# Four single-bank PSUM tiles, another walk over layer 2's odd rows, a pad and another warm-up in an attention and feed-forward kernel

## The chip, the core and the metric

The kernel runs on one core of one Trainium2 chip. The metric is the device time of one execution in microseconds (us), the median of several runs. TensorE (PE) multiplies matrices and writes its results to PSUM, which here has eight banks of 512 fp32 words per partition; VectorE (DVE), ScalarE (ACT) and GpSimd (POOL) do elementwise work, and DVE and ACT empty PSUM; the queue of SyncE (SP) issues the transfers.

## What is computed

```
attention: 4 batches x 8 heads, 576 tokens, head width 64
  scores = q k^T / 8;  keep those >= row max - tau;  softmax over what is kept;  times v
x = the heads side by side                       # 2304 tokens x 512
layer 1: h = x w_in (512 -> 2048); g = h if h >= 1, 0 if h <= -1, else (h + 1)^2 / 4; y = g w_out
layer 2: h = y w_in2 (512 -> 2048); g = s * max(h, 0)^2 + b; out = g w_out2
```

## The kernel before

Every operand of the large matrix products is split into a high and a low part, and each product is done as three matmuls (high by high, high by low, low by high).

A list scheduler that runs on the host writes out the order of all instructions of all engines: each task has engines that may do it, a cost on each, a priority, the tasks that it reads from, and, where it uses PSUM, a group. A group gets a bank when its first product is put in the order and gives it back when its last eviction is. The products of the feed-forward part are also chained in one fixed order on PE ("pe order").

The program has three parts. Attention (to about 500 us) works on half heads: PE makes scores (L576) into double PSUM tiles, DVE takes row maxima (L631), ACT, DVE and POOL do the threshold and the softmax, PE transposes and multiplies by v. Beside and after it the first hidden units of layer 1 are done directly ("plain slices", up to L1018, whose last joins read PSUM). Then come nine steps of three passes over three blocks of 768 tokens: one pass for the second half of layer 1 and two for layer 2.

A step has two halves. gemm1 (L1223) makes eight slices of hidden units for its block from seven products in the order 1, 5, 6, 3, 2, 7, 4 (a scheme of Strassen's type), each 384 columns wide and six matmuls long for each of four pairs of slices. Products are evicted by `copied` (ACT L1127 or DVE L1128) or `joined` (DVE L1131) and shaped by the activation into the slices G, a high and a low part each, in the array pr. gemm2 sums the eight slices into the output: in layer 1 by L1263 (eight groups of 384 columns), in layer 2 by L1299 (six tiles of 128 tokens, 512 columns wide, 6 x 8 x 3 = 144 matmuls for a block, 864 in all). Its rows are the eight slices, first the even ones 0, 2, 4, 6, then the odd ones 1, 3, 5, 7, since gemm1 finishes them in that order; for each row all the tiles are served. In L1299 the stationary operand is G from pr, and the moving one a unit of weights of 2048 bytes in lr, lh or pr; the odd rows read units in lh and pr.

PSUM has two double tiles ps2_0 and ps2_1 (banks 0 to 3), two single tiles ps1_0 and ps1_1 (4 and 5) and a third double tile ps3 (6 and 7), which late in attention is replaced by two single ones. Semaphores guard a whole tile: a write to one half of a double tile waits for reads of the other half, and a read of one half for writes of the other.

At the start nothing can be multiplied until the first inputs land, and PE does matmuls on an identity meanwhile: "fills" (L1397), which the scheduler puts wherever PE would stand idle, and a warm-up of 27 transposes (L781) into ps3 from a copy of the identity that POOL makes.

Of the kernel before, what the change touches and what calls it, by code (L numbers as in the profile page):

```python
# [34 lines left out]
AHEAD = 1  # L35
WARM = 9

# [26 lines left out]
NJ = 4  # L64
BLOCKS = ((0, 768), (768, 768), (1536, 768))
BT = 768
# [18 lines left out]
PR_BYTES = O_EXTRA + UNIT * (NPLACE - NLEFT - NTAIL - NFREE)  # L85
PF_BYTES = 8 * BT


# [263 lines left out]
def mm_ns(n):  # L352
    return 0.443 * n + 5
# [12 lines left out]
def attention_then_ffn(tc, qk, v, tau, w1, w2, s2, b2, out):  # L366
# [53 lines left out]
    ap_ = at_cm.__enter__()  # L420
    ident_r = ap_.tile([128, 128], F32R, name="identr")
    hs_b = [Buf("LF", 1280 * i, TM) for i in range(NH)]
# [9 lines left out]

    ps2 = [pp.tile([128, 2, 512], F32, name=f"ps2_{i}") for i in range(2)]
    ps1 = [pp.tile([128, 512], F32, name=f"ps1_{i}") for i in range(2)]
# [7 lines left out]
    def two_banks():  # L442
        pb["cm"].__exit__(None, None, None)
        pb["cm"] = tc.tile_pool(name="psb", bufs=1, space=bass.MemoryType.PSUM)
        q = pb["cm"].__enter__()
        bank[6:8] = [q.tile([128, 512], F32, name=f"ps4_{i}")[:, :] for i in range(2)]

    E = [ap_.tile([128, S], F32, name=f"e{i}") for i in range(NE)]
# [16 lines left out]
    def consts():  # L465
        make_identity(nc, ident)
        nc.gpsimd.tensor_copy(out=ident_r, in_=ident)
        for c, x in ((half, 0.5), (part_c, 1.0 / S), (tiny_c, 1e-9)):
            nc.vector.memset(c, x)
# [305 lines left out]
    def warm_up():  # L775

        g = Group([(7,)])

        def mm():
            for _ in range(3 * WARM):  # L780
                nc.tensor.transpose(bank[7][:, 0:128].bitcast(F32R), ident_r, ident_r)  # L781

        add([("pool", 1260.0, consts)], (0, 0), w=["ident"])
        add([("pe", WARM * 213.0, mm)], (0, 0), r=["ident"], w=[("bank", g)], group=g)

# [23 lines left out]
    def final():  # L809
        late["md"].__exit__(None, None, None)  # L810
        xg.__exit__(None, None, None)
        late["cm"] = tc.tile_pool(name="final", bufs=1, side="right")
        q = late["cm"].__enter__()
        arena["PR"] = q.tile([128, PR_BYTES // 4], F32R, name="pr")
        arena["PF"] = q.tile([128, PF_BYTES // 4], F32, name="pf")

# [236 lines left out]
    class Pass:  # L1053
# [6 lines left out]
        def product(self, p, j):  # L1060
            return ORDER.index(p) * self.nj + j
# [121 lines left out]
    def gemm1(P, T, first):  # L1183
# [17 lines left out]
        for p in ORDER:  # L1201
# [6 lines left out]
            for j in range(nj):  # L1208
                if p == 1:
                    A[j] = Group(ANY8)  # L1210
                elif p == 5:
                    Bk[j] = Group(ANY8)
# [12 lines left out]

                product(pe, 6 * mm_ns(n), mm, u.keys() + r.keys(), g)
                even, odd = even_b[j], odd_b[j]
# [52 lines left out]
    def gemm2(P, t0, T):  # L1280
# [26 lines left out]
        for i in range(ny):  # L1307
            sums(i)
        for f in rows:
            for i in range(m):  # L1310
                ku = P.unit[P.out(f, 0)].keys() + P.unit[P.out(f, 1)].keys()
                kg = G_b[f].keys(128 * i, 128) + G_b[f].keys(BT + 128 * i, 128)
                product(prs[i][0], 3 * mm_ns(n), lambda f=f, i=i: mm(f, i, gy[i][0]), ku + kg, gy[i][0])
        for i in range(m):
# [50 lines left out]
    layer1 = [t for t in sch.tasks[first:] if t.alts[0][0] != "sp"]  # L1365
    after([t for t in layer1 if t.alts[0][0] == "pe"][:-8], lambda: None, "pe order")
    passes = [Pass(n, layer, f0, nj, 11 * sum(p[2] for p in PASSES[:n])) for n, (layer, f0, nj) in enumerate(PASSES)]
    work = [P.jobs() for P in passes]
# [32 lines left out]
    with tc.manual_schedule():  # L1401
        for t in order:
            t.fn[2]()
    late["cm"].__exit__(None, None, None)
# [66 lines left out]
```

## Time and profile before

| | |
|---|---|
| device time, median of 3 runs | 1081.29 us (1079.51 to 1081.51) |
| device time of the profiled execution | 1079.24 us |
| its span | 1077.4 us |
| PE busy over the span | 1052.1 us (98%), 6491 matmuls |
| DVE busy | 802.2 us (74%) |
| ACT busy | 704.6 us (65%) |
| POOL busy | 428.3 us (40%) |
| DMA, mean over the span | 186 GB/s |

The span is what the hardware profiler saw from the first instruction to the last; the execution's own time is 1.84 us longer. Busy times are those of one execution and overlap between engines.

### The profile page before, as it was taken

The numbers are of one execution on the slowest core, as the hardware profiler recorded it, in microseconds if no ns is written. First come the engines' busy times: TensorE is split into PE (matmuls) and PEld (weight loads), VectorE is DVE, ScalarE is ACT, GpSimd is POOL, SyncE is SP. The second block draws the span as 40 slices with busy tenths as digits, with TensorE's granted clock in tenths as the row PEclk, the third lists the DMA queues.
The fourth block names the chain that finished last, engine by engine and source line by source line (L and its number), as shares of the span: only waits on it lengthen the run. The fifth ranks groups of instructions, "written<-read, shape, count | busy, mean of one in ns | idle before, by whom it ended". The sixth has DMA issues, their size and how long they took to land.

```text
span 1077.4 us, 19033 instructions
## 1 busy us (share of the span) xinstructions
PE 1052.1 (98%) x6491; PEld 925.3 (86%) x6491; DVE 802.2 (74%) x1596; ACT 704.6 (65%) x1322; POOL 428.3 (40%) x653
## 2 busy tenths in 40 slices
PE   9989999999999999999999999999999999999998
PEld 6556877788888898899999999998989889898996
DVE  7988998797887899757888979786796726356372
ACT  7998888898998988734535446265684626346260
POOL 5766767889898978332302111120100101000000
PEclk9999999999999999999999999999999999999999
DMA  5654455565647665599856499843638951140112
GB/s 169 201 156 148 137 184 193 187 199 174 184 137 217 182 198 169 188 355 365 297 173 224 129 307 348 309 168 131 230 128 279 343 174 63 40 137 20 60 30 87
DMA packets 105120, 199.95 MB, mean 186 GB/s; under 512 B 11328, under 2 KB 33344, under 8 KB 105024
## 3 DMA queue, kind: packets, MB, share of 16 engines
q1 hardware_dynamic: 105024, 198.75, 55.9%
q8 instruction: 51, 0.84, 0.3%
q14 instruction: 45, 0.37, 0.1%
HBM read 134.61 MB, written 64.09 MB: 184 GB/s over the span
## 4 chain that ended last, share of the span: by engine, by line
PE 71%; ACT 8%; DVE 6%; issue 2%; POOL 2%; DMA 1%; DVEq 0%; ACTq 0%; POOLq 0%
PE ps L1223 23%; PE ps L1299 18%; PE ps L1263 9%; PE ps L928 5%; PE ps L961 4%; PE ps L695 2%; PE ps L733 2%; PE ps L1009 2%; PE ps L585 2%; ACT p L674 2%; DVE p L639 1%; ACT e L634 1%; ACT pt L687 1%; PE ps L576 1%; PE ps L734 1%
## 5 line engine op out<-in xcount | busy, mean ns | idle before, releaser
L1223 PE MATMUL ps<-pr,lr 128*128 128x384 f32 x816 | 144.7, 336 | 0.0
L1223 PEld LDWEIGHTS ps<-pr,lr 128*128 128x128 f32 x816 | 141.7, 188 | 0.4 <-DVE lg L1131 0.2
L639 DVE SCALAR_TENSOR_TENSOR p<-ps,stt,e 128x576 f32<-128x576 f32 x144 | 116.3, 812 | 21.7 <-ACT e L634 16.8
L1223 PE MATMUL ps<-lr 128*128 128x384 f32 x672 | 122.2, 336 | 0.6 <-DVE lg L1131 0.3
L1223 PEld LDWEIGHTS ps<-lr 128*128 128x128 f32 x672 | 116.7, 188 | 3.1 <-issue 1.4
L631 DVE TENSOR_REDUCE stt<-ps 128x1 f32<-128x576 f32 x144 | 105.8, 749 | 18.2 <-PE ps L585 9.3
L928 PE MATMUL ps<-xh,lr 128*128 128x320 f32 (+1 forms) x512 | 112.6, 299 | 0.2 <-DVE lf L938 0.2
L634 ACT ACTIVATE e<-ps,stt 128x576 f32<-128x576 f32 x144 | 105.9, 751 | 10.4 <-DVE stt L631 9.9
L1299 PE MATMUL ps<-lr,pr 128*128 128x512 f32 x432 | 102.6, 397 | 0.2
L674 ACT ACTIVATE p<-p,stt 128x576 f32<-128x576 f32 (+3 forms) x112 | 93.3, 838 | 12.8 <-DVE stt L658 11.7
L555 DVE TENSOR_TENSOR pr<-lg,pr 128x768 fp32r<-128x768 f32 x71 | 69.2, 978 | 41.6 <-POOL pr L838 26.5
L1299 PEld LDWEIGHTS ps<-lr,pr 128*128 128x128 f32 x432 | 80.5, 188 | 21.0 <-DVE pf L1128 1.4
L1131 DVE TENSOR_TENSOR lg<-lg,ps 128x384 f32<-128x384 f32 (+1 forms) x104 | 56.3, 560 | 47.7 <-PE ps L1299 31.3
L695 PE MATMUL ps<-ident,p 128*128 128x128 f32 x576 | 82.7, 275 | 7.3 <-ACT pt L687 5.2
L928 PEld LDWEIGHTS ps<-xh,lr 128*128 128x128 f32 x512 | 85.1, 188 | 2.9 <-DVE lk L880 0.8
L961 PE MATMUL ps<-g,lr 128*128 128x256 f32 (+1 forms) x600 | 87.1, 297 | 0.0
L687 ACT COPY pt<-ps 128x512 f32<-128x512 f32 x143 | 79.9, 591 | 5.4 <-PE ps L695 5.1
L695 PEld LDWEIGHTS ps<-ident,p 128*128 128x128 f32 x576 | 66.0, 140 | 19.6 <-ACT pt L687 5.5
L1127 ACT COPY lg<-ps 128x384 f32<-128x384 f32 (+1 forms) x107 | 49.3, 494 | 50.8 <-PE ps L1223 44.2
L961 PEld LDWEIGHTS ps<-g,lr 128*128 128x128 f32 x600 | 80.7, 189 | 0.0
L928 PE MATMUL ps<-xl,lr 128*128 128x256 f32 (+1 forms) x256 | 75.3, 294 | 0.0
L733 PE MATMUL ps<-pt,vr 128*64 128x256 f32 (+1 forms) x512 | 69.1, 412 | 0.7 <-ACT pt L687 0.6
(128 smaller groups left out, 2268.1 us busy)
## 6 DMA issues: line engine op xcount, KB each, us to landing
wd<-lh SPq DMA_DIRECT2D x118, 256.0 KB, 4.0
lr<-wd SPq DMA_DIRECT2D x108, 256.0 KB, 5.5
lk<-in_w_dram SPq DMA_DIRECT2D x48, 512.0 KB, 4.5
vr<-in_v_dram SPq DMA_DIRECT2D x32, 320.0 KB, 3.4
r<-in_qk_dram SPq DMA_DIRECT2D x32, 288.0 KB, 3.1
lg<-y1T SPq DMA_DIRECT2D x6, 1536.0 KB, 7.4
lk<-in_w_dram SPq DMA_DIRECT2D x32, 256.0 KB, 3.8
r<-in_qk_dram SPq DMA_DIRECT2D x16, 304.0 KB, 4.2
```

What stands on the lines that cost most here:

```text
L631: add([("dve", 665, lambda: nc.vector.tensor_reduce(out=nm[:, x:x + 1], in_=Sv(), axis=AX.XY, op=ALU.min))], at(pr, "min"), r=[kg], w=[ks[ ...
L634: add([("act", 624, lambda: nc.scalar.activation(out=ev, in_=Sv(), func=AF.Exp, bias=nm[:, x:x + 1], scale=-1.0))], at(pr, "exp"), r=[kg, ...
L639: nc.vector.scalar_tensor_tensor(out=p[:, x * S:x * S + S].rearrange("p (a c) -> p a c", a=2), in0=Sv(), scalar=nthr[:, x:x + 1], in1=ev, ...
L674: nc.scalar.activation(out=p[i:j, o:o + w], in_=p[i:j, a:a + w], func=AF.Identity, scale=rc[i:j, x:x + 1], bias=un[i:j, x:x + 1])
L687: add([("act", actp_ns(n), lambda: [nc.scalar.copy(out=a, in_=b) for a, b in zip(dst, src())]), ("dve", dve_ns(n), lambda: [nc.vector.tens ...
L695: nc.tensor.transpose(bank[g.banks[0]][:, j * 128:(j + 1) * 128], p[:, c0 + j * 128:c0 + (j + 1) * 128], ident)
L733: nc.tensor.matmul(o[64 * x:64 * x + 64, 0:n], vr[:, c:c + D], PT[:, x, k, c0:c0 + n], start=(k == 0), stop=False)
L928: nc.tensor.matmul(o, a, x, start=(n == 0), stop=(n == 11))
L961: nc.tensor.matmul(o, a[:, c], x, start=(f == 0 and n == 0), stop=(f == nf - 1 and n == 2))
L1223: nc.tensor.matmul(o, a, y, start=(i == 0 and p in (1, 5, 2)), stop=(i == 5), skip_group_check=p not in (1, 5, 2))
L1263: nc.tensor.matmul(o, w, x, start=(f == rows[0] and s == 0), stop=(f == rows[-1] and s == 2))
L1299: nc.tensor.matmul(o, a, y, start=(f == rows[0] and s == 0), stop=(f == rows[-1] and s == 2))
```

## The change

It has four parts.

1. The double tiles ps2_0 and ps2_1 get a pool of their own. When the order has come past every task whose group may use a bank below 4 as part of the earlier program (scores, plain slices), `four_banks` closes that pool and opens four single tiles ps5_0 to ps5_3 in the same banks. In the first block, product 1 may only use banks 4 to 7, and product 5 waits for the switch (key "four").
2. In layer 2's gemm2 the even rows are walked as before. The odd rows are walked tile by tile: for each tile of 128 tokens its four odd rows one after the other, twelve matmuls.
3. The array pf is 288 bytes longer. In the built program this moves pr from byte 163808 of each partition to 163520.
4. The warm-up is five fp32 matmuls on the identity itself; its cost in the scheduler's plan stays (1917 ns). The copy of the identity, and its cast on POOL, are gone. Fills that the plan starts before 4500 ns are not written out.

```diff
--- before.py
+++ after.py
@@ -33,7 +33,7 @@
 NSX, NV = 4, 2
 
 AHEAD = 1
-WARM = 9
+WARM, WARM_NS, FILL_FROM = 5, 1917.0, 4500.0
 
 FILL = 200000.0
 NE, NP, NST, NH, LEAD = 2, 3, 4, 3, 3
@@ -84,6 +84,7 @@
 O_EXTRA = 8 * BT * 2 * NJ
 PR_BYTES = O_EXTRA + UNIT * (NPLACE - NLEFT - NTAIL - NFREE)
 PF_BYTES = 8 * BT
+PAD = 288
 
 
 
@@ -418,7 +419,6 @@
     garr = [xp_.tile([128, 2 * TM], F32R, name=f"g{i}") for i in range(NGL)]
     at_cm = tc.tile_pool(name="attn", bufs=1, side="right")
     ap_ = at_cm.__enter__()
-    ident_r = ap_.tile([128, 128], F32R, name="identr")
     hs_b = [Buf("LF", 1280 * i, TM) for i in range(NH)]
     c_b = [Buf("LF", 3840 + 1280 * i, TM) for i in range(NH)]
     ye_b = [Buf("LF", 7680 + 1280 * i, TM) for i in range(2)]
@@ -430,7 +430,9 @@
     yD = dp.tile([NT, DM], F32, name="yd")
     wD = dp.tile([11 * sum(nj for _, _, nj in PASSES), 128, 512], F32, name="wd")
 
-    ps2 = [pp.tile([128, 2, 512], F32, name=f"ps2_{i}") for i in range(2)]
+    pair_cm = tc.tile_pool(name="pairs", bufs=1, space=bass.MemoryType.PSUM, side="right")
+    pairs = pair_cm.__enter__()
+    ps2 = [pairs.tile([128, 2, 512], F32, name=f"ps2_{i}") for i in range(2)]
     ps1 = [pp.tile([128, 512], F32, name=f"ps1_{i}") for i in range(2)]
 
     pb = {"cm": tc.tile_pool(name="psa", bufs=1, space=bass.MemoryType.PSUM)}
@@ -445,6 +447,12 @@
         q = pb["cm"].__enter__()
         bank[6:8] = [q.tile([128, 512], F32, name=f"ps4_{i}")[:, :] for i in range(2)]
 
+    def four_banks():
+        pair_cm.__exit__(None, None, None)
+        late["singles"] = tc.tile_pool(name="singles", bufs=1, space=bass.MemoryType.PSUM, side="right")
+        q = late["singles"].__enter__()
+        bank[0:4] = [q.tile([128, 512], F32, name=f"ps5_{i}")[:, :] for i in range(4)]
+
     E = [ap_.tile([128, S], F32, name=f"e{i}") for i in range(NE)]
     P = [ap_.tile([128, 2 * S], F32, name=f"p{i}") for i in range(NP)]
 
@@ -464,7 +472,6 @@
 
     def consts():
         make_identity(nc, ident)
-        nc.gpsimd.tensor_copy(out=ident_r, in_=ident)
         for c, x in ((half, 0.5), (part_c, 1.0 / S), (tiny_c, 1e-9)):
             nc.vector.memset(c, x)
 
@@ -777,11 +784,11 @@
         g = Group([(7,)])
 
         def mm():
-            for _ in range(3 * WARM):
-                nc.tensor.transpose(bank[7][:, 0:128].bitcast(F32R), ident_r, ident_r)
+            for _ in range(WARM):
+                nc.tensor.matmul(bank[7][:, 0:128], ident, ident, start=True, stop=True)
 
         add([("pool", 1260.0, consts)], (0, 0), w=["ident"])
-        add([("pe", WARM * 213.0, mm)], (0, 0), r=["ident"], w=[("bank", g)], group=g)
+        add([("pe", WARM_NS, mm)], (0, 0), r=["ident"], w=[("bank", g)], group=g)
 
     def attention():
         next_of(prep)
@@ -812,7 +819,7 @@
         late["cm"] = tc.tile_pool(name="final", bufs=1, side="right")
         q = late["cm"].__enter__()
         arena["PR"] = q.tile([128, PR_BYTES // 4], F32R, name="pr")
-        arena["PF"] = q.tile([128, PF_BYTES // 4], F32, name="pf")
+        arena["PF"] = q.tile([128, (PF_BYTES + PAD) // 4], F32, name="pf")
 
     def after(tasks, fn, key, r=()):
         sw = add([("host", 1, fn)], (0, aidx[0] + 1), r=r, w=[key])
@@ -1207,7 +1214,7 @@
             split(T, lambda r=r: r(0, T), lambda r=r: r(BT, T), val[p][0], val[p][1], r.keys(0, T), r.keys(BT, T), sp, pairs_of)
             for j in range(nj):
                 if p == 1:
-                    A[j] = Group(ANY8)
+                    A[j] = Group(ANY if first else ANY8)
                 elif p == 5:
                     Bk[j] = Group(ANY8)
                 g = A[j] if p in (1, 6, 7, 4) else Bk[j] if p in (5, 3) else Group(ANY8)
@@ -1223,7 +1230,7 @@
                             nc.tensor.matmul(o, a, y, start=(i == 0 and p in (1, 5, 2)), stop=(i == 5), skip_group_check=p not in (1, 5, 2))
                             i += 1
 
-                product(pe, 6 * mm_ns(n), mm, u.keys() + r.keys(), g)
+                product(pe, 6 * mm_ns(n), mm, u.keys() + r.keys() + ["four"] * (first and p == ORDER[1]), g)
                 even, odd = even_b[j], odd_b[j]
                 row, at_, n_ = {1: (even, 0, 0), 5: (odd, n, 0), 6: (even, n, 0), 3: (even, n, 1), 7: (odd, n, 1), 2: (even, 0, 1), 4: (odd, 0, 0)}[p]
                 (joined if n_ else copied)(g, n, lambda row=row, at_=at_: row(at_, n), row.keys(at_, n), po)
@@ -1306,11 +1313,12 @@
 
         for i in range(ny):
             sums(i)
-        for f in rows:
-            for i in range(m):
-                ku = P.unit[P.out(f, 0)].keys() + P.unit[P.out(f, 1)].keys()
-                kg = G_b[f].keys(128 * i, 128) + G_b[f].keys(BT + 128 * i, 128)
-                product(prs[i][0], 3 * mm_ns(n), lambda f=f, i=i: mm(f, i, gy[i][0]), ku + kg, gy[i][0])
+        walk = [(f, i) for f in rows[:NJ] for i in range(m)]
+        walk += [(f, i) for i in range(m) for f in rows[NJ:]]
+        for f, i in walk:
+            ku = P.unit[P.out(f, 0)].keys() + P.unit[P.out(f, 1)].keys()
+            kg = G_b[f].keys(128 * i, 128) + G_b[f].keys(BT + 128 * i, 128)
+            product(prs[i][0], 3 * mm_ns(n), lambda f=f, i=i: mm(f, i, gy[i][0]), ku + kg, gy[i][0])
         for i in range(m):
             g, y = gy[i]
             po = prs[i][2]
@@ -1364,6 +1372,7 @@
         l1_out(q, f, f0, f1, gs[n])
     layer1 = [t for t in sch.tasks[first:] if t.alts[0][0] != "sp"]
     after([t for t in layer1 if t.alts[0][0] == "pe"][:-8], lambda: None, "pe order")
+    after([t for t in sch.tasks if t.group is not None and any(min(c) < 4 for c in t.group.cands)], four_banks, "four")
     passes = [Pass(n, layer, f0, nj, 11 * sum(p[2] for p in PASSES[:n])) for n, (layer, f0, nj) in enumerate(PASSES)]
     work = [P.jobs() for P in passes]
     begun = len(sch.tasks)
@@ -1400,7 +1409,9 @@
     order = sch.run()
     with tc.manual_schedule():
         for t in order:
-            t.fn[2]()
+            if t.start >= FILL_FROM or t.alts:
+                t.fn[2]()
+    late["singles"].__exit__(None, None, None)
     late["cm"].__exit__(None, None, None)
     late["lg"].__exit__(None, None, None)
     pb["cm"].__exit__(None, None, None)
```

The order of the instructions changes as follows. At the start of the program, on PE, ps_99 is ps3 (ps_101 after the change), ps_0_92 and ps_1_93 are the double tiles ps2 (ps_0_94 and ps_1_95 after it), and r are the arrays with q and k. Before:

```order
L1397 MATMUL ps_99<-ident 128x128 x4
L781 MATMUL ps_99<-identr 128x128 x27
L1397 MATMUL ps_99<-ident 128x128
L576 MATMUL ps_0_92<-r_111 128x288 x2
L1397 MATMUL ps_99<-ident 128x128
L576 MATMUL ps_1_93<-r_112 128x288 x2
```

With the change, in the same place:

```order
L788 MATMUL ps_101<-ident 128x128 x5
L583 MATMUL ps_0_94<-r_113 128x288 x2
L1406 MATMUL ps_101<-ident 128x128
L583 MATMUL ps_1_95<-r_114 128x288 x2
L583 MATMUL ps_101<-r_113 128x288 x2
```

Four fills, 27 transposes and one more fill ahead of the first score have become five matmuls.

At the end of gemm1 in the second block of layer 1, on PE, ps_0_92 and ps_1_93 are the double tiles, ps_0_94, ps_1_95, ps_0_1148 and ps_1_1149 the single ones. Before:

```order
L1223 MATMUL ps_0_92<-lr 128x384 x12
L1223 MATMUL ps_1_93<-lr 128x384 x12
L1263 MATMUL ps_0_92<-pr,lr 128x384 x6
L1263 MATMUL ps_1_93<-pr,lr 128x384 x6
L1263 MATMUL ps_0_94<-pr,lr 128x384 x3
L1263 MATMUL ps_1_95<-pr,lr 128x384 x3
```

On ACT, which empties these tiles, there stands (L1179 is an activation, L837 a cast of weights or slices):

```order
L1127 COPY lg<-ps_0_92 128x384 x2
L1127 COPY pf<-ps_1_93 128x384
L1179 ACTIVATE lf<-lf,cst 128x768
L1127 COPY pf<-ps_1_93 128x384
L837 CAST pr<-lg 128x768
```

With the change, ps_0_5873 to ps_3_5876 are the four new tiles, and PE has:

```order
L1230 MATMUL ps_0_5873<-lr 128x384 x6
L1230 MATMUL ps_1_5874<-lr 128x384 x6
L1230 MATMUL ps_2_5875<-lr 128x384 x6
L1230 MATMUL ps_3_5876<-lr 128x384 x6
L1270 MATMUL ps_0_5873<-pr,lr 128x384 x3
L1270 MATMUL ps_1_5874<-pr,lr 128x384 x3
L1270 MATMUL ps_2_5875<-pr,lr 128x384 x3
L1270 MATMUL ps_3_5876<-pr,lr 128x384 x3
```

and ACT:

```order
L1134 COPY lg<-ps_0_5873 128x384
L1134 COPY lg<-ps_1_5874 128x384
L1134 COPY pf<-ps_2_5875 128x384
L1186 ACTIVATE lf<-lf,cst 128x768
L1134 COPY pf<-ps_3_5876 128x384
```

The sequence of products and evictions is the same; each now has a tile of its own.

At the end of the program, on PE, ps_0_92 and ps_1_93 are the double tiles, ps_0_94 and ps_1_95 single ones. Before:

```order
L1299 MATMUL ps_0_92<-pr 128x512 x6
L1299 MATMUL ps_1_93<-pr 128x512 x6
L1299 MATMUL ps_0_94<-pr 128x512 x3
L1299 MATMUL ps_1_95<-pr 128x512 x3
L1299 MATMUL ps_0_92<-pr 128x512 x6
L1299 MATMUL ps_1_93<-pr 128x512 x6
L1299 MATMUL ps_0_94<-pr 128x512 x3
L1299 MATMUL ps_1_95<-pr 128x512 x3
```

With the change, where ps_0_96 and ps_1_97 are the same single tiles:

```order
L1306 MATMUL ps_0_96<-lh,pr 128x512 x4
L1306 MATMUL ps_0_96<-pr 128x512
L1306 MATMUL ps_0_96<-lh,pr 128x512
L1306 MATMUL ps_0_96<-pr 128x512 x6
L1306 MATMUL ps_1_97<-lh,pr 128x512 x4
L1306 MATMUL ps_1_97<-pr 128x512
L1306 MATMUL ps_1_97<-lh,pr 128x512
L1306 MATMUL ps_1_97<-pr 128x512 x6
```

The last two rows for all six tiles have become the twelve odd-row matmuls of the last two tiles.

## Rows read from the trace of the kernel before

**Rows 1.** Window of the feed-forward part: us, PE, PEld, DVE, ACT, POOL busy, PEclk, DMA share, GB/s.

```profile
505.00:1072.80 567.80, 565.04 (x2942) 521.48 (x2940) 384.18 (x588) 283.53 (x448) 64.67 (x67) 1.00 0.52 177
```

**Rows 2.** Timeline of PE (start us, us), and L1263's group (busy us, mean ns, idle).

```profile
593.71 2.76 PE L1223 MATMUL ps<-lr 128*128 128x384 f32 x15
596.31 1.20 PE L1263 MATMUL ps<-pr,lr 128*128 128x384 f32 x6
598.25 3.04 PE L1263 MATMUL ps<-pr,lr 128*128 128x384 f32 x16 [0.73 <-ACT pf L1127]
...
533.36 2.87 PE L1263 MATMUL ps<-pr,lr 128*128 128x384 f32 x15 [0.47 <-ACT pf L1127]
...
785.48 2.35 PE L1223 MATMUL ps<-lr 128*128 128x384 f32 x12 [0.27 <-DVE pf L1131]
...
724.21 6.12 PE L1299 MATMUL ps<-lr,pr 128*128 128x512 f32 x24
...
850.40 4.81 PE L1299 MATMUL ps<-lr,pr 128*128 128x512 f32 x18
...
L1263 PE MATMUL ps<-pr,lr 128*128 128x384 f32 x288 | 51.1, 337 | 1.9 <-ACT pf L1127 1.9
```

**Rows 3.** Timeline of ACT at the stall of 597 us.

```profile
596.51 0.48 ACT L1127 COPY pf<-ps 128x384 f32<-128x384 f32 x1 [1.22 <-PE ps L1223]
...
597.72 0.47 ACT L1127 COPY pf<-ps 128x384 f32<-128x384 f32 x1
```

**Rows 4.** Timeline of the first feed-forward block: DVE and PE.

```profile
502.48 1.68 DVE L1018 TENSOR_TENSOR md<-ps,md 128x320 f32<-128x320 f32 x4
...
502.99 4.32 PE L1223 MATMUL ps<-lr 128*128 128x384 f32 x24
```

**Rows 5.** Timeline of PE in the last block, and PE's groups by shape.

```profile
1039.74 16.48 PE L1299 MATMUL ps<-lr,pr 128*128 128x512 f32 x70
...
1064.46 8.36 PE L1299 MATMUL ps<-pr 128*128 128x512 f32 x36
...
L1223 PE MATMUL ps<-pr,lr 128*128 128x384 f32 x816 | 144.7, 336 | 0.0
L1223 PE MATMUL ps<-lr 128*128 128x384 f32 x672 | 122.2, 336 | 0.6 <-DVE lg L1131 0.3 <-DVE pf L1131 0.3
L1299 PE MATMUL ps<-lr,pr 128*128 128x512 f32 x432 | 102.6, 397 | 0.2
L1299 PE MATMUL ps<-pr 128*128 128x512 f32 x252 | 64.4, 391 | 0.0
...
L1299 PE MATMUL ps<-lh,pr 128*128 128x512 f32 x180 | 48.8, 396 | 0.0
```

**Rows 6.** Timeline where the odd rows of layer 2's first block begin.

```profile
741.07 0.95 DVE L555 TENSOR_TENSOR pr<-pf,pr 128x768 fp32r<-128x768 f32 x1
...
741.36 2.03 PE L1299 MATMUL ps<-lh,pr 128*128 128x512 f32 x8
```

**Rows 7.** The end: timeline of DVE, and how long L1318's transfers took to land.

```profile
1072.70 1.28 DVE L1131 TENSOR_TENSOR lg<-lg,ps 128x512 f32<-128x512 f32 x2
...
DMA to landing us min/median/max: 2.0/2.1/2.4
```

**Rows 8.** Timeline of the start: PE, ACT and DVE.

```profile
1.34 2.08 PE L1397 MATMUL ps<-ident 128*128 128x128 f32 x8 [1.34 <-POOL ident masks.py:199]
...
3.07 3.23 PE L781 MATMUL ps<-identr 128*128 128x128 f32 x25
3.39 0.42 ACT L513 ACTIVATE r<-r 128x256 f32<-128x256 f32 x1 [1.39 <-DMA r<-in_qk_dram]
5.60 0.42 ACT L513 ACTIVATE r<-r 128x256 f32<-128x256 f32 x1 [1.79 <-DMA r<-in_qk_dram]
...
6.70 0.76 PE L576 MATMUL ps<-r 64*128 64x288 f32 x4
...
8.60 0.76 DVE L631 TENSOR_REDUCE stt<-ps 128x1 f32<-128x576 f32 x1 [0.34 <-PE ps L576]
```

## The prediction

> **What bounds the kernel now.** I read the feed-forward part (505 us to the last matmul) first, as one window: PE is busy 565.04 of 567.80 us there, with 2942 matmuls, at a granted clock of 1.00, while DVE, ACT and POOL have 384, 284 and 65 us and the DMA share is 0.52 [rows 1]. So three things only can shorten this part: fewer matmuls (the change has the same number), less time from one matmul's start to the next, and the few stalls between them. Then I read the costliest groups of PE by shape, for the spacing, the timeline of PE at its stalls, for what it waits for, and the timelines of both ends of the run, where PE isn't yet or no longer the bound. A group's mean is the time of one pipelined matmul and is longer than the spacing; spacing is start to start. In a row of n matmuls it is (length − one matmul)/(n − 1), or the step from one row's start to the next over the count.
>
> **Four single tiles for two double ones.** In the second layer-1 block the 15 matmuls that begin at 593.71 are followed at 596.31, so 384-wide matmuls come every 2.60/15 = 0.1733 us. Six of L1263 begin at 596.31 and should be followed at 597.35; the next begins at 598.25, 0.90 us late. The row calls 0.73 of it idle [rows 2], since 0.17 is hidden under the end of the matmul before. It waits for an ACT eviction: one runs 596.51 to 596.99, the other 597.72 to 598.19 [rows 3]. By the order of ACT both empty the same double tile, and the second stands behind an activation. The first half's product was done six matmuls (1.04 us) before the second's, but its eviction began only at 596.51, after PE's last write to the *other* half. PE in turn wanted the first half and waited for the eviction of the second. With a tile for each bank the first eviction can begin at about 595.4; an activation of 0.9 us follows, and the second eviction ends at about 597.4. PE wants that bank after nine matmuls of L1263 instead of six, at 596.31 + 9 × 0.1733 = 597.87, so 0.5 us of cover are left.
>
> Which stalls are of this kind I took from the order of both programs: waits of PE for the eviction of another half than the one it writes. There are 57 in the feed-forward part before and none after; most are met long before. Those that show: 533.36 has 0.47 idle, so 0.47 + 0.17 = 0.64 late; 598.25, 0.90; the third layer-1 block has the same 0.73 of idle (all of L1263's 1.9 us are 0.47 + 0.73 + 0.73), 0.90; 785.48, 0.27 + 0.17 = 0.44 [rows 2]. Two lie inside rows of 512-wide matmuls: 24 from 724.21 take 6.12 us where 23 × 0.2330 (the spacing of such rows, worked out with the pad) + 0.40 = 5.76, so 0.36; 18 from 850.40 take 4.81 where 17 × 0.2330 + 0.40 = 4.36, so 0.45 [rows 2]. Together 3.69. Behind a stall the first matmuls are slower: 16 from 598.25 take 3.04 where 15 × 0.1733 + 0.34 = 2.94, 0.1 us, four times. **−4.1 us.** Bounds: −2.0, if half of these waits are replaced by one for the right bank, and −5, if waits that follow from these go too (waits for the right bank stay as they are).
>
> The new tiles cost no instruction but a wait: product 5 of the first block waits for "four", the last reader of a bank below 4. That is DVE's L1018, which runs 502.48 to 504.16, while PE has 24 matmuls of product 1 from 502.99 to 507.31 [rows 4], on banks 4 to 7. Behind the waiting matmul stands all of PE, but the wait has been met 3 us before; without this cover it would cost up to 1.2 us, once. **0.**
>
> **The pad.** In the built program lr, lh and pr begin at bytes 17088, 122560 and 163808 of a partition, that is 704, 704 and 992 modulo 1024; the change moves pr to 163520, which is 704 as well. Layer 2's 512-wide matmuls read G from pr (stationary) and a weight unit (moving) from lr, lh or pr. With lr they come every (16.48 − 0.40)/69 = 0.2330 us, with pr every (8.36 − 0.39)/35 = 0.2277; the means of the groups differ likewise, 397 for lr, 396 for lh, 391 for pr [rows 5]. 432 + 180 = 612 matmuls are of the slow kind. If the phase between the two operands is the reason, they become like the 252: 612 × 0.0053 = 3.2 us by the spacing, 612 × 0.006 = 3.7 by the means. **−3.7 us**, since the spacing comes from two rows and the means from all 864. The 384-wide ones won't change: 672 with both operands in lr, hence at one phase, and 816 with one in pr have the same mean, 336 [rows 5]. Bounds: 0, as one contrast (pr against lr and lh) can't tell the phase from the place, and −4.3 (0.007, as far as the means are rounded).
>
> A page speaks against this term: the Trainium skill, "TensorE: Matmul & The Clock Gate", section "Step-by-step: what each phase is for", has PE read the streaming operand and the weights through two independent ports, so that loading the next weights takes nothing from the running matmul. By that rule no phase between the two can matter and the pad is worth 0. That the rows above differ by 5 to 6 ns with nothing but the place of an operand changed doesn't fit it well.
>
> **Odd rows tile by tile.** Same 864 matmuls in layer 2. Before, each step of an odd row served six tiles, and the fourth odd slice was wanted last; now tile 0 wants all four in its first twelve matmuls, its fourth about 2.1 us after the odd rows begin. In the tightest block odd rows begin at 741.36 and the last odd slice is made by DVE until 741.07 + 0.95 = 742.02 [rows 6], wanted at 743.46, or 742.6 when matmuls before it come faster: 0.6 us of cover, 1 to 3 in the others. **0**; each us that a slice is late costs one. The ring that product 5 reads shares a slice that comes free a little later, 3 us before it is filled.
>
> At the end two joins follow the last matmuls, 1072.70 to 1073.98 (two of 0.64), since the last two tiles end almost together, and the landing of the last result takes 2.4 us against a median of 2.1 and a minimum of 2.0 [rows 7]. Tile by tile, only one join of 0.64 follows PE's end, and the transfers before it have left: 0.45 to 0.64 of join and 0 to 0.4 of landing. **−0.7 us** (−0.4 to −1.0).
>
> **Warm-up.** PE does four fills of 0.43 us from 1.34, then 27 transposes from 3.07 to 6.31 and the first score at 6.70 [rows 8]. The operand of that score was scaled at 3.39 + 0.42 = 3.81, that of the second at 5.60 + 0.42 = 6.02 [rows 8]. So PE's own warm-up holds the first score back, by 2.9 us. Now five matmuls of 0.43 end at 1.34 + 2.16 = 3.50, the first score begins at about 3.9 and the second at about 6.05, behind its operand. How fast PE is so early no row gives: the score's four matmuls take 0.76 at 6.70, and I allow twice that at 3.9, the ratio of the clock's two levels of 1.2 and 2.4 GHz, though the view calls the granted clock 1.00 from the start on. So the first score ends near 5.4 where it ended at 7.46, and the second, from 6.05, near 7. DVE's reduction of the second began at 8.60 [rows 8]; that is some 1.6 us earlier. POOL's cast of the identity goes as well, off the path. Attention hands its work in rings from PE to DVE, ACT and POOL, so a shift goes on to its end, less what later transfers take back, which don't come earlier; I take a quarter off. **−1.2 us.** Bounds: −2.1 (the shift of the first score's end) and 0.
>
> **Sum.** 4.1 + 3.7 + 0.7 + 1.2 = 9.7 us. The profiled execution took 1079.24 us, its span 1077.4; from it, 1069.5. It lies 2.05 below the median of the runs shown, 1081.29, and inside their spread, so the same 9.7 off the median give 1071.6, which I take.
>
> **Rivals.** *The pad does nothing*: what counts is where the moving operand lies. For: lr and lh are slow, pr fast, and no other place for G is in the trace. Against: 32 or 0 modulo 64 alone makes no difference at 384 wide. 9.7 − 3.7 = 6.0: 1075.3.
> *The waits go elsewhere*: four single evictions per product instead of two pairs fall on an ACT that does activations between them, and PE waits for the right bank half as long: −9.7 + 2.1: 1073.7. Against: the 0.5 us of cover worked out above.
> *The start gives nothing*: PE pauses between the first two scores and stays slow over more of them, or the loads hold attention at its old pace: 9.7 − 1.2 = 8.5, 1072.8.
> *Odd slices come late*: 0.5 us in each of six blocks of layer 2, +3: 1074.6. Against: cover in every block.
> *Slower*: the pad puts pr where it meets lr and lh badly. The 384-wide matmuls that mix them (816 in L1223, 288 in L1263 and, by its order, 120 more with lh) and the 252 of layer 2 that are fast now then take the 0.006 us more that layer 2's mixed ones take before: 1476 × 0.006 = 8.9, less the other terms' 6.0, +2.9: 1084.2. It decides from 6.0/0.006 = 1000 matmuls on. Against: the pairs within pr and within lr are at that phase already, and are the fast ones or no slower.
>
> **How the numbers follow.** The likeliest case, all four terms near their values, has 0.64, and by itself 1069 to 1074. The pad at nothing has 0.17, waits elsewhere 0.07, a poor start 0.05, late slices 0.04, slower 0.03 (half of it within 0.2% of no change). About 0.2%, 2.2 us, is what a measurement of this kernel can tell from no change. All cases but the last lie more than that below 1081.29: faster 0.95, same 0.02, slower 0.03. The range reaches from 1067.2 (waits −5, pad −4.3, start −2.1, end −1.0 make −12.4, 1068.9, and 1.7 for the runs' own spread) up to the pad's case and 1.3 above it, 1076.6.
>
> **What would show it.** Waits: no idle on ACT or DVE evictions at the first nine matmuls of L1263's line in the three layer-1 blocks, and the feed-forward part's idle down from 2.8 to under 1.5 us. Pad: all 512-wide groups at a mean near 391 and a spacing near 0.227; if only pr's group is there, the term is 0. Walk: one join behind the last matmul, and PE without a wait on DVE's or POOL's slices where odd rows begin. Warm-up: the first score at 3.9, the first feed-forward matmul 1 to 1.5 us earlier. Wrong would make it a shift of the attention part by another amount, since its order is the same but its waits are close, or 384-wide groups off 336.

## The result, and the profile after

The changed kernel took 1069.99 us (median of 4, 1068.99 to 1070.44) against 1080.74 us before (median of 4): a ratio of 0.990, 95% interval 0.9883 to 0.9917. On another chip it took 1069.66 against 1081.56, ratio 0.9887 (0.987 to 0.9904). Forecast were 1071.6 us and a range of 1067.2 to 1076.6. The profiled execution took 1070.16 us with a span of 1068.4, 9.0 less than that of before. The sum came out nearly right, its terms less so.

The feed-forward part, as a window from its first matmul to the end of its last; first of before, then of the changed kernel. Columns as in [rows 1].

```profile
502.99:1072.82 569.83, 567.07 (x2954) 523.49 (x2952) 386.21 (x591) 284.77 (x451) 65.41 (x68) 1.00 0.52 178
```

```profile
505.75:1064.48 558.73, 558.59 (x2954) 523.94 (x2952) 387.06 (x580) 288.42 (x454) 70.14 (x76) 1.00 0.53 183
```

It is 11.1 us shorter with as many matmuls, and PE's idle time in it fell from 2.76 us to 0.14. But it begins 2.8 us *later* than before, not 1.2 earlier. From the last matmul's end to the span's end it takes 3.9 us instead of 4.6.

PE's groups by shape, in the changed kernel. They answer to [rows 5] and to L1263's row in [rows 2].

```profile
L1230 PE MATMUL ps<-pr,lr 128*128 128x384 f32 x816 | 144.2, 334 | 0.0
L1230 PE MATMUL ps<-lr 128*128 128x384 f32 x672 | 121.2, 334 | 0.1
L1306 PE MATMUL ps<-lr,pr 128*128 128x512 f32 x432 | 99.1, 390 | 0.0
L1306 PE MATMUL ps<-pr 128*128 128x512 f32 x252 | 68.8, 389 | 0.0
L1270 PE MATMUL ps<-pr,lr 128*128 128x384 f32 x288 | 50.4, 334 | 0.0
...
L1306 PE MATMUL ps<-lh,pr 128*128 128x512 f32 x180 | 52.5, 389 | 0.0
```

L1270's idle of 1.9 us is gone, and the three 512-wide groups now agree within 1 ns: lr 397 to 390, lh 396 to 389, and pr, which was 391, is 389 too. The 384-wide groups went from 336 and 337 to 334.

The place of [rows 2, 3] in the second block of layer 1, PE and ACT of the changed kernel by time:

```profile
594.75 3.11 PE L1230 MATMUL ps<-lr 128*128 128x384 f32 x17
597.70 4.49 PE L1270 MATMUL ps<-pr,lr 128*128 128x384 f32 x25
...
596.86 0.48 ACT L1134 COPY pf<-ps 128x384 f32<-128x384 f32 x1 [0.56 <-PE ps L1230]
597.24 0.94 ACT L1186 ACTIVATE lf<-lf,cst 128x768 f32<-128x768 f32 x1
598.08 0.47 ACT L1134 COPY pf<-ps 128x384 f32<-128x384 f32 x1
```

L1270's 25 matmuls run in one piece. The first eviction begins 0.84 us before L1270 does (0.20 after L1263's start in [rows 3]); the second ends at 598.55, and PE wants its bank at 597.70 + 9 × 0.1733 = 599.26. The cover is 0.7 us, where 0.5 was worked out.

The start, by time, answering to [rows 8]:

```profile
1.34 2.50 PE L788 MATMUL ps<-ident 128*128 128x128 f32 x10 [1.34 <-POOL ident masks.py:199]
3.56 0.42 ACT L520 ACTIVATE r<-r 128x256 f32<-128x256 f32 x1 [1.56 <-DMA r<-in_qk_dram]
4.03 1.24 PE L583 MATMUL ps<-r 64*128 64x288 f32 x4 [0.18 <-ACT r L520]
...
6.02 0.42 ACT L520 ACTIVATE r<-r 128x256 f32<-128x256 f32 x1 [2.04 <-DMA r<-in_qk_dram]
6.49 1.24 PE L583 MATMUL ps<-r 64*128 64x288 f32 x8 [0.80 <-ACT r L520]
7.29 0.76 DVE L638 TENSOR_REDUCE stt<-ps 128x1 f32<-128x576 f32 x1 [1.22 <-PE ps L583]
```

The first score begins at 4.03, the second waits for its operand until 6.49, and the second reduction begins at 7.29 instead of 8.60: 1.3 us earlier, where 1.6 was worked out. So in this execution the start did nearly what was forecast. Where the gain went is seen further on, in PE's rows of scores: of before,

```profile
58.35 0.76 PE L576 MATMUL ps<-r 64*128 64x288 f32 x4
...
73.99 0.76 PE L576 MATMUL ps<-r 64*128 64x288 f32 x4
```

and the same matmuls of the changed kernel,

```profile
57.30 0.76 PE L583 MATMUL ps<-r 64*128 64x288 f32 x4
...
75.84 0.76 PE L583 MATMUL ps<-r 64*128 64x288 f32 x4
```

1.05 us ahead at the first, 1.85 behind at the second: 2.9 us are lost in between. Windows of that stretch, before and then changed; the column before the DMA share is the granted clock:

```profile
64.00:66.00 2.00, 1.00 (x10) 0.76 (x8) 1.80 (x5) 2.00 (x5) 1.71 (x5) 1.00 1.03 374
66.00:68.00 2.00, 0.92 (x7) 0.52 (x6) 1.70 (x4) 2.00 (x6) 1.57 (x3) 1.00 0.08 28
68.00:70.00 2.00, 2.00 (x17) 0.98 (x17) 1.82 (x8) 1.99 (x7) 1.04 (x3) 1.00 0.15 42
```

```profile
63.00:65.00 2.00, 1.00 (x9) 0.76 (x8) 1.80 (x5) 2.00 (x5) 1.75 (x4) 1.00 0.95 327
65.00:67.00 2.00, 0.96 (x7) 0.52 (x6) 1.75 (x4) 2.00 (x6) 1.53 (x3) 0.87 0.08 25
67.00:69.00 2.00, 2.00 (x8) 1.10 (x8) 1.09 (x6) 1.80 (x5) 0.87 (x2) 0.50 0.17 47
...
71.00:73.00 2.00, 2.00 (x8) 1.02 (x10) 1.17 (x5) 1.98 (x5) 0.73 (x1) 0.50 0.53 145
```

Both have the same sparse stretch, in which PE is half idle waiting for ACT's evictions of transposes. In the changed kernel's execution the clock then goes to the lower of its two levels (0.50, that is 1.2 GHz) until 73.3; in the other it doesn't.

### The profile page after: what moved, and what is told of

Its sections match the earlier page's. It is cut to its first block, busy times and chain, and to the rows that moved or that the text cites. A ratio compares the mean times of both kernels' runs of the same rounds, so it can differ in the third digit from the quotient of the medians.

```text
span 1068.4 us, 19016 instructions
## 1 busy us (share of the span) xinstructions
PE 1044.9 (98%) x6464; PEld 924.2 (86%) x6464; DVE 802.4 (75%) x1585; ACT 708.3 (66%) x1325; POOL 434.5 (41%) x660
## 4 chain that ended last, share of the span: by engine, by line
PE 71%; ACT 7%; DVE 5%; POOL 3%; issue 2%; DMA 1%; DVEq 0%; POOLq 0%; ACTq 0%; SPq 0%
PE ps L1230 24%; PE ps L1306 18%; PE ps L1270 9%; PE ps L935 5%; PE ps L968 4%; PE ps L702 2%; PE ps L740 2%; PE ps L1016 2%; ACT p L681 2%; PE ps L592 2%; DVE p L646 1%; ACT e L641 1%; ACT pt L694 1%; PE ps L583 1%; POOL lr L561 1%
## 5 line engine op out<-in xcount | busy, mean ns | idle before, releaser
L1306 PE MATMUL ps<-lr,pr 128*128 128x512 f32 x432 | 99.1, 390 | 0.0
L1134 ACT COPY lg<-ps 128x384 f32<-128x384 f32 (+1 forms) x113 | 55.4, 493 | 60.3 <-PE ps L1230 41.6
L845 POOL CAST pr<-lf 128x768 fp32r<-128x768 f32 x6 | 5.0, 831 | 166.8 <-PE ps L1306 116.6
```

The lines of the kernel that those rows point to most:

```text
L1306: nc.tensor.matmul(o, a, y, start=(f == rows[0] and s == 0), stop=(f == rows[-1] and s == 2))
```

## The experiments

The executions of one kernel differ by up to 5.8 us, in part by the clock of this stretch, so each comparison below also has the mean granted clock that every execution reports. Executions with a mean of 0.999 or 1.00 are called *even* here. Of 58 executions of the kernel before whose clock is known, 31 were even; of the changed kernel's ten, three. On the chip of the first four experiments the even ones of before took 1079.2 us on average and the others 1082.5; on the three other chips the even ones took 1080.3 to 1080.9. Even executions of one kernel on one chip still differ, by up to 2.4 us in the kernel before and up to 3.5 in one below. What the parts do inside the feed-forward part is read from traces, where the clock is 1.00.

**The warm-up alone** (before, with part 4 of the change).

```diff
-            for _ in range(3 * WARM):
-                nc.tensor.transpose(bank[7][:, 0:128].bitcast(F32R), ident_r, ident_r)
+            for _ in range(WARM):
+                nc.tensor.matmul(bank[7][:, 0:128], ident, ident, start=True, stop=True)
```

> The kernel before with the new warm-up alone. Theory: the first scores come 1.2 us earlier, as in the changed kernel's trace, but the same sparse stretch of PE at 63 to 67 us is again followed by a granted clock of 0.5 for some 6 us, and layer 1's blocks begin 2.8 us later than before: about 1083.5 us against 1080.7. Rival: the late attention of the changed kernel is an accident of its one profiled execution or comes from another part; then the start's 1.2 us stay and this kernel takes about 1079.5, with a granted clock of 1.00 throughout.

Measured: 1081.42 against 1081.45, ratio 1.0005 (0.9993 to 1.0017); 4 of 12 even, these at 1079.7 on average, where the even ones of before took 1079.2. So alone it gained nothing, and both expectations were too simple. The profiled execution has a mean clock of 0.999 and no fall, and yet its first feed-forward matmul comes at 503.70, 0.7 us later than before: it lost the start's gain early. Its fills:

```profile
8.42 2.50 PE L1395 MATMUL ps<-ident 128*128 128x128 f32 x10
```

Ten of these take 1.38 us at 7.66 in the changed kernel's trace. Here PE kept the pace of its first microseconds to about 10.9 us. That it isn't this kernel alone shows in the changed kernel with the old walk (below), which has the changed kernel's start:

```profile
9.02 2.07 PE L1405 MATMUL ps<-ident 128*128 128x128 f32 x10
```

What the start gives depends on when PE reaches its full pace, and that varies between executions. In the five traces with the new warm-up the 21st matmul record of the scores begins at 11.7 to 11.9 us in three and at 13.8 and 13.9 in two; in the nine with the old one, at 12.9 to 13.9. So the gain is 1 us or more in three of five, and nothing in two.

**The pad alone**, and two others: `PAD = 288`, `PAD = 256` and `PAD = 32`, each the only edit to the kernel before.

```diff
-        arena["PF"] = q.tile([128, PF_BYTES // 4], F32, name="pf")
+        arena["PF"] = q.tile([128, (PF_BYTES + PAD) // 4], F32, name="pf")
```

> The kernel before with the pad of 288 bytes alone. Theory: layer 2's 612 matmuls that read a unit of lr or lh go from 0.2333 to 0.227 us, all three groups of L1299's line have means of 389 to 391 ns, everything else stays: 3.9 us less, about 1076.8. Rival (two independent read ports, so no phase between the operands matters; the changed kernel's spacing comes from its other walk or its tiles): no change, 1080.7, group means 397, 396, 391.

> The kernel before with a pad of 256 bytes, alone: pr moves nearly as far as with 288, to byte 163552 (736 modulo 1024, where lr and lh are at 704). Theory (the phase between the two operands counts, and must be equal): 612 matmuls stay at 0.2333 us, no change. Rival (the place of pr in the partition counts, or the distance): 4.2 us less, as with 288.

> The kernel before with a pad of 32 bytes, alone: pr at 163776, a multiple of 64 as lr and lh are, but 960 modulo 1024 where they are at 704. If it is enough that both operands have the same phase modulo 64, layer 2's mixed matmuls go to 0.227 us and 4.2 us are gained; if the phase must be the same in larger units (256, 512 or 1024), they stay at 0.2333 and nothing is gained. I hold the first for likelier, 2 to 1.

Measured: 288 bytes, 1076.07 against 1081.45, ratio 0.9958 (0.9942 to 0.9974); 256 bytes, 1080.42 against 1081.56, 0.9992 (0.9981 to 1.0003); 32 bytes, 1075.13 against 1081.56, 0.9944 (0.993 to 0.9958). Layer 2's groups, first with 288 bytes, then with 256, then with 32:

```profile
L1300 PE MATMUL ps<-lr,pr 128*128 128x512 f32 x432 | 100.1, 391 | 0.2
L1300 PE MATMUL ps<-pr 128*128 128x512 f32 x252 | 63.9, 389 | 0.0
L1300 PE MATMUL ps<-lh,pr 128*128 128x512 f32 x180 | 47.6, 389 | 0.0
```

```profile
L1300 PE MATMUL ps<-lr,pr 128*128 128x512 f32 x432 | 102.6, 397 | 0.1
L1300 PE MATMUL ps<-pr 128*128 128x512 f32 x252 | 64.4, 391 | 0.0
L1300 PE MATMUL ps<-lh,pr 128*128 128x512 f32 x180 | 48.9, 396 | 0.0
```

```profile
L1300 PE MATMUL ps<-lr,pr 128*128 128x512 f32 x432 | 100.1, 391 | 0.2
L1300 PE MATMUL ps<-lh,pr 128*128 128x512 f32 x180 | 47.6, 389 | 0.0
```

What counts is the distance between the two operands: 32 bytes, after which pr lies a multiple of 256 from lr and lh, do all of it, and 256, which move pr eight times as far and keep that distance off by 32, nothing. lr and lh didn't move and became fast, so it isn't the place of the moving operand; and the 252 within pr, whose stationary operand moved as well, changed by 2 ns only, so it isn't the stationary operand's place alone either. The expectation for 32 bytes was wrong on what it tells apart: 960 and 704 are equal modulo 256, so it excludes that the two must be equal modulo 512 or 1024, and leaves open whether 64, 128 or 256 is the unit.

With the pad of 288 a row of lh comes every (4.47 − 0.39)/18 = 0.2267 us, before (2.03 − 0.40)/7 = 0.2329 [rows 6], and the 384-wide matmuls gained a little too:

```profile
1054.82 4.47 PE L1300 MATMUL ps<-lh,pr 128*128 128x512 f32 x19
...
L1224 PE MATMUL ps<-pr,lr 128*128 128x384 f32 x816 | 144.5, 334 | 0.0
L1264 PE MATMUL ps<-pr,lh 128*128 128x384 f32 x120 | 24.6, 334 | 0.0
```

Before, the last two have 144.7 and 336 [rows 5], and 24.8 and 337; with 256 bytes they stay at 336 and 338.

**The four tiles alone** (part 1 of the change).

```diff
-    ps2 = [pp.tile([128, 2, 512], F32, name=f"ps2_{i}") for i in range(2)]
+    ps2 = [pairs.tile([128, 2, 512], F32, name=f"ps2_{i}") for i in range(2)]
...
+        bank[0:4] = [q.tile([128, 512], F32, name=f"ps5_{i}")[:, :] for i in range(4)]
```

> The kernel before with the four single tiles alone (old walk, old warm-up, no pad). Theory: all the stalls that the changed kernel lost in its feed-forward part, 6.3 us and the slow matmuls behind them, are the tiles', also those that wait for the right bank: 7 us less, about 1073.7, and the feed-forward part's idle near 0.4. Rival: only the waits for the other half go, 4.1 us, about 1076.6, and the rest of the stalls needs the new walk.

Measured: 1072.38 against 1081.45, ratio 0.993 (0.9914 to 0.9947); the four even executions took 1071.9 on average, 7.3 less than those of before. Its feed-forward window:

```profile
503.65:1067.00 563.35, 563.21 (x2954) 524.34 (x2952) 388.10 (x591) 287.78 (x451) 61.01 (x68) 1.00 0.52 180
```

569.83 − 563.35 = 6.5 us, and 0.14 of idle is left. So the theory's size holds, and the new walk isn't needed for it. Its reason doesn't: what went beyond the forecast 4.1 wasn't waits for the right bank, but more waits for the other half (see the section on why the prediction was right).

**The new walk alone** (part 2).

```diff
-        for f in rows:
-            for i in range(m):
+        walk = [(f, i) for f in rows[:NJ] for i in range(m)]
+        walk += [(f, i) for i in range(m) for f in rows[NJ:]]
+        for f, i in walk:
```

> The kernel before with the new walk over layer 2's odd rows alone. Theory: only the end gets shorter, one join less behind the last matmul: 0.7 us less, about 1080.0, stalls at the ends of the blocks as before. Rival: the walk frees the tiles one by one at a block's end, and the stalls where layer 2's products wait for the right bank go too: 3 us less, about 1077.7.

Measured: 1093.45 against 1081.45, ratio 1.0123 (1.0103 to 1.0143). Neither was right; alone it costs 12 us. Its feed-forward window:

```profile
507.06:1090.71 583.65, 571.20 (x2954) 522.83 (x2952) 386.41 (x580) 284.98 (x454) 72.01 (x76) 1.00 0.51 176
```

PE is idle for 12.5 us of it. PE and ACT by time, in the odd rows of the first block of layer 2:

```profile
749.18 0.86 PE L1299 MATMUL ps<-lh,pr 128*128 128x512 f32 x3
750.72 0.50 PE L1299 MATMUL ps<-lh,pr 128*128 128x512 f32 x1 [0.68 <-ACT lg L1127]
...
750.08 0.59 ACT L1127 COPY lg<-ps 128x512 f32<-128x512 f32 x1 [1.51 <-PE ps L1299]
```

Tile 0 is finished at about 749.4 and its eviction could begin, but the other half of its double tile is tile 1, whose first three matmuls stand ahead of the eviction in the order. ACT waits for them until 750.08, and tile 1's fourth matmul waits for ACT until 750.7. The next matmul should start at 749.18 + 3 × 0.233 = 749.88: 0.84 us, and 0.1 for the slower one behind it. If it is as much at both double tiles in all six blocks, that makes 12 × 0.94 = 11.3 of the 13.8 us by which the window is longer. So the tiles are what allows the walk.

**The changed kernel with the old walk** (the same edit, taken back).

> The changed kernel with the old walk over layer 2's odd rows. Theory: with the four single tiles the walk changes only the end, so two joins stand behind the last matmul again: the end takes 4.6 us from PE's last matmul on where it takes 3.9, 0.7 us more, and the feed-forward part keeps its 558.4. Rival: the new walk also frees tiles earlier for the next block, and stalls come back without it: 2 us more.

Measured: 1069.10 against 1081.31, ratio 0.9888 (0.9875 to 0.9902), with the walk 0.9887. Its end, PE and DVE:

```profile
1057.68 6.51 PE L1306 MATMUL ps<-pr 128*128 128x512 f32 x28
1060.83 1.36 DVE L1138 TENSOR_TENSOR lg<-lg,ps 128x512 f32<-128x512 f32 x2 [15.07 <-PE ps L1306]
...
1063.55 1.37 DVE L1138 TENSOR_TENSOR lg<-lg,ps 128x512 f32<-128x512 f32 x2
```

and that of the changed kernel:

```profile
1062.95 1.52 PE L1306 MATMUL ps<-pr 128*128 128x512 f32 x6
...
1064.52 0.69 DVE L1138 TENSOR_TENSOR lg<-lg,ps 128x512 f32<-128x512 f32 x1 [2.03 <-PE ps L1306]
```

Without the new walk DVE's last join ends 1064.92 − 1064.19 = 0.73 us after PE; with it 1065.21 − 1064.47 = 0.74; before, 1073.98 − 1072.82 = 1.16 [rows 7, 5]. With single tiles the six joins begin earlier (3.4 us ahead of PE's end, before 2.7), so no queue of them stands behind the last matmul either way. On top of the tiles the walk is worth 0.3 us at most: the feed-forward window is 559.01 us long without it and 558.73 with it, and the ratios agree.

**The changed kernel again, and with the old warm-up** (part 4 taken back).

> The changed kernel once more, beside the next three on one chip. In half of the executions so far, of every kernel, the granted clock falls to 0.5 for some 6 us near 66 to 74 us, and these take 2 to 4 us longer. Theory: so it is here too: about 1069.5 where the mean clock is 0.999 or 1.00, 1070.5 to 1072 where it is below, a median near 1070.5.

> The changed kernel with the old warm-up. Theory: the tiles (6.5 us), the pad (4.2) and the last join (0.65) make the whole gain, and the new warm-up gives nothing that lasts beyond the first 25 to 70 us: 1079.1 less 11.4, about 1067.7, in executions with a mean clock of 0.999 or more, that is 0 to 2 us below the changed kernel. Rival: the warm-up's 1.2 us, which the changed kernel's trace shows up to 67 us, stay where the clock doesn't fall; then this kernel takes 1.2 us more than the changed one.

Measured: 1069.66 (one of six even, 1066.56) and 1070.33 (one of five even, 1067.39), ratios 0.9887 (0.987 to 0.9904) and 0.9891 (0.9875 to 0.9907) on the same chip. Inconclusive: the clock's fall hides a term of 1 us, and the two even executions, 0.8 apart, are one of each.

**PE kept busy in the sparse stretch**: transposes that wait there for their eviction are done again into the same bank, in the changed kernel, in the kernel before, and in the changed kernel with the old warm-up.

```diff
+    def again(t):
+        if t.fn[0] != "pe" or not t.alts or not 62000.0 < t.start < 65000.0 or t.group.banks != (5,):
+            return 1
+        return {109: 6, 436: 3}.get(int(t.fn[1]), 1)
...
-                t.fn[2]()
+                for _ in range(again(t)):
+                    t.fn[2]()
```

> The changed kernel with PE kept busier at 63 to 67 us: two groups of transposes that wait there for their eviction are done again into the same bank, five and eight more matmuls, where PE stood idle. Theory: the fall of the granted clock at 66 to 74 us follows on this sparse stretch; without it the clock stays at 1.00 and every execution is like the best one of the changed kernel, 1066.6 us, so a median near 1067 against 1069.7. Rival: the falls come by themselves, and some in ten executions keep them: a median near 1069.7, or later by up to 1 us if the repeated transposes hold an eviction back.

> The kernel before with the same repeated transposes alone. Theory: no fall of the clock, all executions near the 1079.2 that its undisturbed ones took, against a median of 1081.5. Rival: as before, a median near 1081.5 with mean clocks of 0.996 to 0.998 in half of the executions.

> The changed kernel with the old warm-up and with the repeated transposes at 63 to 67 us, so that the clock doesn't fall and the warm-up's own worth can be seen. Theory: the new warm-up is worth the 1.2 us that the traces show from the first blocks of attention on, so this kernel takes about 1068.6 where the one with the new warm-up took 1067.4, with a mean clock of 0.999 or 1.00 in every execution. Rival: the start's gain is lost again before layer 1 in most executions: about 1067.4 here too.

Measured: 1067.47 (1066.58 to 1067.73, 4 of 4 even), ratio 0.9875 (0.986 to 0.989); 1082.0 against 1081.31 (11 of 11 even), 0.9999 (0.999 to 1.0009); 1068.52 (5 of 5 even), 0.9877 (0.9859 to 0.9895). Windows of the first of the three:

```profile
63.00:65.00 2.00, 1.55 (x14) 1.31 (x13) 1.69 (x5) 2.00 (x6) 1.78 (x4) 1.00 0.95 344
65.00:67.00 2.00, 1.55 (x13) 1.18 (x11) 1.85 (x4) 1.86 (x5) 1.41 (x3) 1.00 0.05 19
67.00:69.00 2.00, 1.96 (x17) 1.07 (x17) 1.60 (x7) 1.99 (x7) 0.73 (x3) 1.00 0.19 61
```

In all 20 executions of the three the clock held, so the fall does follow on the sparse stretch. For the changed kernel this is the best version: its four executions lie below nine of the changed kernel's ten, though those ran on other chips and the two ratios' intervals overlap. In the kernel before it gained nothing: its 1081.6 us on average are 0.7 above the even executions of before on that chip (1080.9), about what the better clock had saved. Its profiled execution (1082.54) loses 1.6 us at one place of the feed-forward part, where the kernel before waits too, but not so that the profile shows it:

```profile
595.50 4.40 PE L1223 MATMUL ps<-lr 128*128 128x384 f32 x24 [1.60 <-DVE lg L1131]
```

Whether the other ten lose it there, and why, stayed open. Between the first and the third the warm-up makes 1.05 us, near the 1.2 forecast; they ran on different chips and their executions overlap, so this bears it out and doesn't settle it. Their two traces have the same feed-forward window (558.77) and no fall, and enter it at 502.12 and 504.88, so the whole difference is attention's; but with the old warm-up and no repeats the changed kernel's trace, without a fall too, enters it at 502.87, so most of the 2.8 us isn't the warm-up's.

## Why the prediction was right, and where its terms were off

*Four tiles*: forecast −4.1, measured −6.5 in the feed-forward part. The mechanism was right: an eviction of a single bank begins as soon as its own product is done (0.84 us ahead of L1270 instead of 0.20 behind L1263), and no wait for another half is left. The term was mis-sized at "Those that show": the list is short. One that it leaves out shows as idle, in [rows 5] as L1223's 0.3 for lg and here by time:

```profile
653.75 2.07 PE L1223 MATMUL ps<-pr,lr 128*128 128x384 f32 x11
656.15 4.41 PE L1223 MATMUL ps<-lr 128*128 128x384 f32 x24 [0.34 <-DVE lg L1131]
```

By the order PE writes the first half of ps2_0 there and waits for DVE's join of the second; it begins 0.50 us late. Others are hidden under the end of the matmul before and show no idle at all. Read from start to start, with the halves taken from the order, the trace of before has 13 late starts that wait for another half, 4.67 us together, where the list's six make 3.4. Behind each of the 13 a matmul is about 0.1 us slower, 1.2 in all, where the prediction counted "four times". That is 5.9 of the 6.5, and with it the term went beyond its bound of −5. "Waits for the right bank stay as they are" was not the error: there are three short ones before, 0.5 with the slow matmuls behind them, and one of 0.3, with 0.1 behind it, in the changed kernel.

*The pad*: forecast −3.7, measured −4.55 (569.83 − 565.28, where the second is the same window with the pad alone). The phase between the operands was the reason, to a multiple of 256 bytes as far as was tested. The 612 matmuls alone gave what was forecast: by the means 432 × 0.006 + 180 × 0.007 = 3.85, by the steps from start to start, summed over both traces, 3.75. The size was low because the 252 within pr, which alternate with those of lh, gained as well (0.46 by their steps), and because the 384-wide ones that mix pr with lr or lh did (0.35). "The 384-wide ones won't change" was wrong: their means fell from 336 and 337 to 334 and 335. The rival that ended slower feared the opposite and had nothing to it. The rival of two independent ports falls here: by the rule that the prediction took from the Trainium skill ("TensorE: Matmul & The Clock Gate", "Step-by-step: what each phase is for") a pad of 32 bytes would have been worth nothing, and it gave 0.56%.

The two add up: 6.5 + 4.55 = 11.0, and the changed kernel's window is 11.1 shorter.

*The odd rows*: no odd slice was late, as forecast (PE's idle of 0.14 leaves no room), and the end is 0.7 shorter, as forecast. But the 0.7 was put down to the walk, and the tiles do it: with them alone the end takes 1071.0 − 1067.0 = 4.0 us, 0.6 less than before. The step "Tile by tile, only one join of 0.64 follows PE's end" missed that two joins stood there because they were late, not because the tiles end together.

*The warm-up*: forecast −1.2, and 1.05 to 1.3 us are there in the changed kernel's rows to 57 us. Alone it gave nothing, and in two of five traces PE stayed slow to 10.5 and 10.9 us: the rival "The start gives nothing", held at 0.05, had this right. The step that failed is "so a shift goes on to its end": what the start gives isn't there in each execution, and a later event can take it. The prediction saw a start that stays slow; it didn't see a clock that falls later, after a stretch that the change doesn't touch and that the trace of before passes at 1.00. This fall cost 2.9 us in the profiled execution.

So the sum, 9.7, met the measured 10.75 by errors of opposite sign, which is luck: 3.2 us more from tiles and pad, against a start that often gives nothing and falls of the clock in seven of the changed kernel's ten executions and in 27 of 58 of before. Without falls, and with nothing for the warm-up, the terms as measured make 6.5 + 4.55 + 0.7 = 11.75 us off the even executions of before, 1079.2 to 1080.9 by chip: 1067.4 to 1069.1. The changed kernel's three even executions took 1066.56, 1068.99 and 1069.81. What moves the even ones by some 3 us lies in attention, whose length differs so between the traces without a fall, and wasn't pinned down further.

## What to carry to other kernels

Give each PSUM bank a tile of its own where PE is the bound: the halves of one tile wait for each other, and that can cost more than the idle time in the trace suggests (2.8 us of idle here, 6.5 of gain; and a walk that is free with single tiles cost 12 us with double ones). Look for such waits from start to start, since a short one hides under the matmul before. Compare the spacing of like matmuls by the place of their operands; 6 ns over 612 matmuls were had here for 32 bytes. When executions of one kernel differ by some us, look at the granted clock by windows before believing any term of that size.

## What the runs showed of the hardware

- A 512-wide matmul of layer 2 whose two operands lie a multiple of 256 bytes apart follows its predecessor after 0.2267 us (the row of lh with the pad of 288); 32 bytes off that, after 0.2330 [rows 5]. Whether 64 or 128 bytes would do wasn't tested. At 384 columns the means differ by 2 to 3 ns, and the window by 0.35 us over 1224 matmuls.
- The granted clock fell to 0.50 behind a stretch of 4 us with PE busy for 1.96, for 6.8 us in four traces and 3.4 in one. The mean clock was lower in 62 of 124 executions without the repeated transposes, and in none of 20 with them (PE busy for 3.10 in the profiled one).
- Behind each of the 13 late starts of the kernel before PE's next matmul came 0.08 to 0.11 us late as well.
- In the first microseconds the profile gives a granted clock of 1.00 while ten fill matmuls take 2.50 us, against 1.38 later; in two of five traces with the new warm-up they keep that pace to 10.5 and 10.9 us. The pace there is read from durations.
